# Turning the first x block by DMA in single tiles, with the v rows of wqkv on the other DMA queue, v of eight tiles tile by tile, and wk turned in two parts

## The chip, the core and the metric

The kernel runs on one core of a Trainium2 chip. The metric is device time in microseconds (us); a figure for a kernel is the median of its runs.

"Turn" below means a DMA that transposes on its way (DMA_TRANSPOSE in the profile). A "tile" of x is 128 tokens by 640 values, 160 KB. A "v piece" is 128 rows of the 640 v columns of wqkv, also 160 KB; v of one token tile needs all five pieces. SP is the sync engine, whose queue issues most DMAs.

## The reference

```python
def reference(A_x, A_wqkv, A_w_phi, A_wo, B_x, B_w_gate, B_w_up, B_w_down, gate_w):
    # S = 2048 tokens, D = 640, 32 heads of 20, F = 1728, all bf16
    def _A_ref(x, wqkv, w_phi, wo):
        ...                                   # q, k, v = x @ wqkv
        pq = jnp.einsum("bhsd,hdf->bhsf", q, w_phi)
        pk = jnp.einsum("bhsd,hdf->bhsf", k, w_phi)
        phi_q = concatenate([softmax(pq), softmax(-pq)])
        phi_k = concatenate([softmax(pk), softmax(-pk)])
        ...                                   # linear attention, then @ wo
    def _B_ref(x, w_gate, w_up, w_down):
        return (_gelu(x @ w_gate) * (x @ w_up)) @ w_down
    x = A_x
    g = _sigmoid((x * gate_w).sum(-1, keepdims=True))
    return g * _A_ref(x, A_wqkv, A_w_phi, A_wo) + (1 - g) * _B_ref(x, ...)
```

(Shortened; the attention's den has a term of 1e-6.) Only the first 30 of some 290 us matter here: x has to be turned, so that the model dimension lies on partitions; v is x times the v columns of wqkv; and the kernel folds w_phi into wk and wq, for which it needs those turned too.

## The kernel before

A small scheduler issues instructions in program order on each engine and adds the semaphore waits. The loads at the start, with cuts:

```python
    def loads(self):
        ...
        def xload(q, j):      # two tiles of x, tokens on partitions, as they lie in memory
            sc.dma(q, lambda e: e.dma_start(self.xtok[:, j:j + 2, :], x4[:, j:j + 2, :]), ...)
        def wload(T, c0, key):
            sc.dma("sp", lambda e: e.dma_start_transpose(T[:, :, :], self.wqkv[:, c0:c0 + D]), writes=[key])
        def xturn(t, n):
            a, z = t * P, (t + n) * P
            sc.dma("sp", lambda e: e.dma_start_transpose(self.xT[:, :, a:z], self.x[a:z, :]), ...)
        ...
        xload("sp", 0)
        xload("act", 2)
        ...                                            # wphi, on act
        for kt in range(KD):                           # the five v pieces
            sc.dma("sp", lambda e: e.dma_start(self.w3[:, kt, 0:D], w3[:, kt, 2 * D:3 * D]), writes=[("wv", kt)])
        ...                                            # gate column, on act
        xturn(4, 2)
        wload(self.wkT, D, "wkT")
        xturn(6, 2)
        wload(self.wqT, 0, "wqT")
        xturn(8, 4)
        xturn(12, 4)
        ...                                            # then the FFN weights
```

The first four tiles of x are turned by the PE, and their v is computed piece by piece: the first v piece for all four tiles, then the second, and so on, so that the last piece is needed last.

```python
    def attention_state(self):
        ...
        warm(7)                                        # dummy matmuls on a zeroed tile
        xt(0, 6, "d"); xt(1, 7, "a"); xt(2, 2, "d"); xt(3, 3, "a")   # PE transposes, evacuated by DVE or ACT
        for t in range(4): vs(t, 0)                    # vs(t, kt): v piece kt for tile t
        ...                                            # the same for pieces 1, 2, 3
        self.blockdiag()
        self.gate_column(6)
        for t in range(4):
            vs(t, 4)
            ...                                        # evacuations
        f = self.fold
        self.v_early(4, 6)                             # all five pieces for one tile
        self.v_early(5, 0)
        f(0, "k", (2, 3), "d")                         # fold of wk: needs the turned wk
        f(1, "k", (4, 5), "a")
        self.v_early(6, 6)
        f(2, "k", (2, 3), "d"); f(3, "k", (4, 5), "a"); f(4, "k", (0, 1), "d")
        self.v_early(7, 6)
        self.k_early(0, 2)
        f(0, "q", (4, 5), "d")                         # fold of wq: needs the turned wq
        ...
        self.pq(0, 1, 1); self.pq(0, 0, 0); self.pq(0, 3, 3)         # bank 6 + n % 2
        ...
```

The softmax here doesn't subtract the row's maximum and nothing guards it: scores larger than these inputs give would overflow.

## Time and profile before

| | before |
|---|---|
| time | 289.78 us, median of 3 (289.63 to 290.26); 289.85 with three more |
| span of the profiled run | 288.7 us |
| first fold of wk / of wq on the PE | 15.25 / 20.98 us |
| v pieces land (five) | 5.3, 6.4, 6.8, 7.2, 7.7 us |
| turned wk / wq lands | 12.2 / 18.9 us |

Landing times are the start of a DMA's issue plus the time from issue to landing that the profile gives for it, good to about 0.1 us.

The profile page, its first lines: busy us of each engine, share of the span, instructions.

```profile
span 288.7 us, 7036 instructions
PE 284.0 (98%) x3032; PEld 190.1 (66%) x3032; DVE 166.7 (58%) x337; ACT 105.1 (36%) x199; POOL 27.6 (10%) x52
```

The PE is busy nearly everywhere and nothing else bounds the kernel, so what counts in the start is when the PE gets through it. The PE's timeline of the start (start us, duration us, engine, line, operation, out<-in, count, and in brackets the idle time before and what ended it):

```profile
4.72 2.31 PE L290 MATMUL ps<-ident,xtok 128*128 128x128 bf16 x20 [0.30 <-DMA xtok<-in_A_x_dram]
6.82 4.73 PE L363 MATMUL ps<-w,xT 128*128 128x480 bf16 x32
...
11.45 1.25 PE L363 MATMUL ps<-w,xT 128*128 128x480 bf16 x8
12.53 2.88 PE L351 MATMUL ps<-w,xT 128*128 128x512 bf16 x20
15.25 0.79 PE L331 MATMUL ps<-BD,wkT 128*128 128x140 bf16 x12
...
20.98 0.79 PE L331 MATMUL ps<-BD,wqT 128*128 128x140 bf16 x12
```

L290 are the PE transposes, L363 v of tiles 0 to 3, the twenty at 12.53 v of tiles 4 and 5, L331 the folds. The last has 2.0 us to spare on the turned wq.

The timeline of the sync queue (the duration is the time the queue needs to issue):

```profile
0.80 0.41 SPq L216 DMA_DIRECT2D xtok<-in_A_x_dram  x1
1.27 2.43 SPq L233 DMA_DIRECT2D w<-in_A_wqkv_dram  x5
3.75 2.11 SPq L224 DMA_TRANSPOSE xT<-in_A_x_dram  x1
5.91 3.71 SPq L220 DMA_TRANSPOSE wkT<-in_A_wqkv_dram  x1
9.66 1.41 SPq L224 DMA_TRANSPOSE xT<-in_A_x_dram  x1
11.11 4.25 SPq L220 DMA_TRANSPOSE wqT<-in_A_wqkv_dram  x1
```

It has no pause: everything that is turned stands in one line, and wq comes after 9 blocks of 160 KB.

The table of stretches (us from:to, length; busy us and instructions of each engine; then the recorded PE clock, the DMA engines' busy share, GB/s). The share sums the times of all packets that start in the stretch, so it can exceed 1. The clock column reads 1.00 also where a trace holds no clock record, as this one: its 480-column matmuls took 524 ns at 6.82 us and 366 ns from 7.25 us, so the clock was not full before about 7 us.

```profile
core 0: us, PE busy (x) PEld busy (x) DVE busy (x) ACT busy (x) POOL busy (x), PEclk, DMA share, GB/s
2.00:4.00 2.00, 2.00 (x6) 0.59 (x4) 0.00 (x0) 1.28 (x1) 1.52 (x11) 1.00 0.95 325
4.00:6.00 2.00, 1.70 (x14) 1.29 (x14) 0.49 (x1) 0.00 (x0) 1.59 (x12) 1.00 1.09 323
6.00:8.00 2.00, 2.00 (x17) 1.42 (x16) 1.47 (x6) 1.41 (x2) 1.12 (x8) 1.00 1.23 224
```

Plain loads move 325 GB/s until 6 us. The waits of the PE near 29 us (waiting engine, for what: total us, times, longest):

```profile
PE ps L351 <- ACT Eq L518: 0.3, 1, 0.3
```

That is a q projection that waits for PSUM bank 7.

### The profile page before, as it was taken

The page shows a single profiled execution, that of the slowest core. Times are in us where ns is not written, and L with a number is a line of the kernel's source. Part 1 is how long each engine was busy: PE and PEld are TensorE (multiplying, and loading weights), DVE is VectorE, ACT ScalarE, POOL GpSimd, SP SyncE. Part 2 cuts the span into 40 slices and gives each one's busy share as a digit, 9 for nine tenths or more (in the row PEclk, how much of TensorE's full clock was granted, in tenths as well). Part 3 has the DMA queues.
Part 4 walks back from the last instruction along what each step waited for, and adds up shares of the span by engine and source line. Part 5 has one row for each costly group of instructions (what it writes and reads, how often), then busy time and mean ns, then how long its engine had stood idle before and what let it go on. Part 6 is the DMA issues. An engine that isn't in the chain of part 4 may idle for free.

```text
span 288.7 us, 7036 instructions
## 1 busy us (share of the span) xinstructions
PE 284.0 (98%) x3032; PEld 190.1 (66%) x3032; DVE 166.7 (58%) x337; ACT 105.1 (36%) x199; POOL 27.6 (10%) x52
## 2 busy tenths in 40 slices
PE   7999999999999999999999999999999999999996
PEld 4576689999994444444688744457764444777785
DVE  2338999999977553777776443326744232674001
ACT  2357897687663322322111332220132222022111
POOL 7000000000000000111113200001230000113000
DMA  8999994000002000011212120000312000031211
GB/s 225 217 192 293 361 356 119 0 2 2 0 2 48 0 0 0 3 25 31 25 37 70 28 66 0 3 0 15 80 25 68 0 2 0 2 92 26 70 49 49
DMA packets 36938, 18.68 MB, mean 65 GB/s; under 512 B 28970, under 2 KB 36394, under 8 KB 36906
## 3 DMA queue, kind: packets, MB, share of 16 engines
q1 hardware_dynamic: 36096, 17.86, 23.8%
q8 instruction: 24, 0.39, 0.6%
q10 hardware_dynamic: 810, 0.35, 0.5%
q14 instruction: 8, 0.07, 0.1%
HBM read 9.04 MB, written 2.62 MB: 40 GB/s over the span
## 4 chain that ended last, share of the span: by engine, by line
PE 97%; DMA 1%; ACT 1%; issue 0%; ACTq 0%
PE ps L351 61%; PE ps L708 28%; PE ps L651 2%; PE ps L363 2%; PE ps L449 2%; DMA xtok<-in_A_x_dram 1%; PE ps L331 1%; PE ps L290 1%; ACT Ek L413 0%; ACT Eq L518 0%; ACT outsb L721 0%; ACT gcol L416 0%; PE ps L313 0%; ACTq L42 0%
## 5 line engine op out<-in xcount | busy, mean ns | idle before, releaser
L708 PE MATMUL ps<-wd_sb,hT 64*128 64x320 bf16 (+2 forms) x918 | 67.6, 288 | 0.0
L625 DVE TENSOR_TENSOR hT<-ps,gl 128x512 bf16<-128x512 f32 x52 | 35.7, 690 | 55.1 <-PE ps L351 54.9
L351 PE MATMUL ps<-xT,wg_sb 128*128 128x512 bf16 (+1 forms) x270 | 64.9, 379 | 0.0
L351 PE MATMUL ps<-xT,wu_sb 128*128 128x512 bf16 (+1 forms) x270 | 64.8, 379 | 0.0
L623 ACT ACTIVATE gl<-ps 128x512 bf16<-128x512 f32 x52 | 30.9, 597 | 71.5 <-PE ps L351 64.9
L708 PEld LDWEIGHTS ps<-wd_sb,hT 64*128 64x128 bf16 x918 | 46.0, 94 | 13.2 <-ACT gl L623 0.8
L351 PEld LDWEIGHTS ps<-xT,wu_sb 128*128 128x128 bf16 (+1 forms) x270 | 26.5, 99 | 29.7 <-DVE hT L625 0.4
L680 POOL TENSOR_TENSOR Og<-O,O 128x640 bf16<-128x640 bf16 x16 | 22.3, 1395 | 237.3 <-DVE O L678 237.3
L351 PEld LDWEIGHTS ps<-xT,wg_sb 128*128 128x128 bf16 (+1 forms) x270 | 25.9, 99 | 28.7 <-issue 0.5
L351 PE MATMUL ps<-w,xT 128*64 128x512 bf16 (+6 forms) x400 | 42.1, 325 | 0.0
L721 ACT ACTIVATE outsb<-ps,Gm 128x320 bf16<-128x320 f32 (+2 forms) x31 | 14.6, 516 | 74.8 <-PE ps L708 74.8
L351 PEld LDWEIGHTS ps<-w,xT 128*64 128x64 bf16 (+1 forms) x400 | 35.9, 107 | 4.7
L708 PE MATMUL ps<-wo_sb,goT 64*128 64x320 bf16 (+2 forms) x340 | 28.2, 288 | 0.0
L351 PE MATMUL ps<-xT,wq 128*64 128x512 bf16 (+1 forms) x185 | 26.4, 380 | 0.3 <-ACT Eq L518 0.3
L433 DVE TENSOR_TENSOR Ek<-Ek,Dk 128x640 bf16<-128x640 bf16 x32 | 25.0, 821 | 0.5
L678 DVE TENSOR_TENSOR O<-ps,RH 128x640 bf16<-128x640 f32 x32 | 24.8, 815 | 0.0
L424 DVE TENSOR_REDUCE Dk<-Ek 128x64 f32<-128x1280 bf16 x16 | 23.7, 1478 | 0.2 <-ACT gcol L416 0.2
L518 ACT ACTIVATE Eq<-ps 128x512 bf16<-128x512 f32 x40 | 21.7, 604 | 1.1 <-PE ps L351 0.8
L413 ACT ACTIVATE Ek<-ps 128x640 bf16<-128x640 f32 x32 | 20.7, 702 | 3.5 <-PE ps L351 3.5
L708 PEld LDWEIGHTS ps<-wo_sb,goT 64*128 64x128 bf16 x340 | 17.7, 94 | 4.7
L351 PEld LDWEIGHTS ps<-xT,wq 128*64 128x64 bf16 (+1 forms) x185 | 15.3, 108 | 3.5 <-ACT Eq L518 0.8
L667 DVE RECIPROCAL RH<-ps 128x32 f32<-128x32 f32 x16 | 5.7, 358 | 18.3 <-PE ps L651 18.3
(65 smaller groups left out, 151.1 us busy)
## 6 DMA issues: line engine op xcount, KB each, us to landing
out_dram<-outsb SPq DMA_DIRECT2D x7, 320.0 KB, 2.4
wd_sb<-in_B_w_down_dram SPq DMA_DIRECT2D x1, 2080.0 KB, 13.6
wg_sb<-in_B_w_gate_dram SPq DMA_DIRECT2D x1, 1120.0 KB, 6.0
wu_sb<-in_B_w_up_dram SPq DMA_DIRECT2D x1, 1120.0 KB, 8.5
wg_sb<-in_B_w_gate_dram SPq DMA_DIRECT2D x1, 960.0 KB, 9.7
wu_sb<-in_B_w_up_dram SPq DMA_DIRECT2D x1, 960.0 KB, 10.2
w<-in_A_wqkv_dram SPq DMA_DIRECT2D x5, 160.0 KB, 4.4
wo_sb<-in_A_wo_dram SPq DMA_DIRECT2D x1, 800.0 KB, 9.4
```

The lines of the kernel that those rows point to most:

```text
L351: self.sc.op("pe", lambda e: e.matmul(self.ps[a:z, bank * 512 + c0:bank * 512 + c0 + n], lhs[:, a:z], rhs, start=first, stop=fin), reads=r ...
L363: sc.op("pe", lambda e, c0=c0, n=n, bk=bk, col=col: e.matmul(self.bank(bk)[:, col:col + n], self.xT[:, kt, t * P:(t + 1) * P], self.w3[:, ...
L413: self.sc.op("act", lambda e, s=s, scale=scale: e.activation(self.Ek[:, se, s, :], self.ps[:, o:o + self.D], AF.Exp, scale=scale), reads=[ ...
L424: sc.op("dve", lambda e: e.tensor_reduce(self.Dk[:, se, 0, :].rearrange("p (s h) -> p s h", h=H), self.Ek[:, se, :, :].rearrange("p s (h d ...
L433: sc.op("dve", lambda e, v=v, r=r: e.tensor_tensor(v, v, r, ALU.mult), reads=[("Rk", se)], writes=[("Ek", se, s)])
L518: sc.op("act", lambda e, s=s, scale=scale: e.activation(self.Eq[:, s, i, b * self.BT:(b + 1) * self.BT], self.bank(bank), AF.Exp, scale=sc ...
L623: sc.op("act", lambda e: e.activation(self.gl[:, slot, :], self.bank(banks[0]), AF.Gelu_apprx_tanh), reads=[("ps", banks[0])], writes=[("g ...
L625: sc.op("dve", lambda e: e.tensor_tensor(hT[:, c, :], self.bank(banks[1]), self.gl[:, slot, :], ALU.mult), reads=[("ps", banks[1]), ("gl", ...
L678: dve(lambda e, o=o, f=f, s=s: e.tensor_tensor(o, V[s][:, :, :, 0:DH], f, ALU.mult), rb + [key(6 + s)], [("O", s, sl)], guard=old)
L680: sc.op("pool", lambda e: e.tensor_tensor(self.Og[:, sl, :], self.O1[:, sl, :], self.O2[:, sl, :], ALU.add), reads=[("O", 0, sl), ("O", 1, ...
L708: sc.op("pe", lambda e: e.matmul(self.bank(bk, w), lhs, rhs, start=opens and x == 0, stop=end and not opens, skip_group_check=True), reads ...
L721: sc.op("act", lambda e: e.activation(dst, self.bank(bk, w), AF.Copy, scale=g), reads=rd, writes=wr)
```

## The change

The intent: take the PE transposes and their evacuations (2.31 us of PE time) out of the start by letting the DMA turn the first x tiles too, singly so that the first arrives early; load the v pieces from the ACT queue at the same time; and split wk's turn so that x tiles 6 and 7 come between its parts. One early q projection also moves from PSUM bank 7 to bank 0. The diff, cut to its core (removed helpers, an order of memsets, an output layout, the number of semaphores of the ACT queue and book-keeping keys are left out):

```diff
-        xload("sp", 0)
-        xload("act", 2)
+        for kt in range(KD):
+            sc.dma("act", lambda e: e.dma_start(self.w3[:, kt, 0:D], w3[:, kt, 2 * D:3 * D]), writes=[("wv", kt)])
         ... wphi, on act
-        for kt in range(KD):
-            sc.dma("sp", lambda e: e.dma_start(self.w3[:, kt, 0:D], w3[:, kt, 2 * D:3 * D]), writes=[("wv", kt)])
         ... gate column, on act
+        xturn(0, 1)
+        xturn(1, 1)
+        xturn(2, 2)
         xturn(4, 2)
-        wload(self.wkT, D, "wkT")
+        wload(self.wkT, D, "wkT", 0, 2)
         xturn(6, 2)
-        wload(self.wqT, 0, "wqT")
+        wload(self.wkT, D, "wkT", 2, 5)
+        wload(self.wqT, 0, "wqT", 0, 5)
 ...
-        warm(7)                    # on a tile that the DVE clears first
-        xt(0, 6, "d")  ...         # PE transposes of tiles 0 to 3
-        for t in range(4): vs(t, 0)  ...
+        for i in range(8):         # dummy matmuls on the constant ones
+            sc.op("pe", lambda e: e.matmul(self.bank(7), ones[:, 0:P], ones, start=True, stop=True), writes=[("ps", 7)])
+        f = self.fold
         self.blockdiag()
+        for t in range(5):
+            self.v_early(t, 2 * t % 8)
+        self.gate_column(2)
+        self.v_early(5, 6)
 ...
-        self.pq(0, 3, 3)
+        self.pq(0, 3, 3, 0)
```

More of the change, by code (lines that the diff above doesn't have):

```diff
@@ L135, in run @@
         self.columns = False
-        self.sc = _Sched(nc, {"sp": (nc.sync, 16), "act": (nc.scalar, 4), "pool": (nc.gpsimd, 2)})
+        self.sc = _Sched(nc, {"sp": (nc.sync, 16), "act": (nc.scalar, 8), "pool": (nc.gpsimd, 2)})
         self.loads()
@@ L156, in alloc @@
         self.ident = T("ident", [P, P], BF16)
-        self.zero = T("zero", [P, 512], BF16)
         self.gz = T("gz", [P, P], BF16)
@@ L194, in alloc @@
         place([
-            [("xtok", [P, self.TB, D], BF16), ("wkT", [P, KD, D], BF16), ("wqT", [P, KD, D], BF16)],
+            [("wkT", [P, KD, D], BF16), ("wqT", [P, KD, D], BF16)],
             [("goT", [P, 8, KD, P], BF16), ("O1", [P, 2, D], BF16), ("O2", [P, 2, D], BF16),
@@ L211, in loads, with wload @@
         w3 = self.wqkv.rearrange("(kt p) n -> p kt n", p=P)
-        x4 = self.x[0:self.BT, :].rearrange("(p j) n -> p j n", j=self.TB)
-        def xload(q, j):
-            sc.dma(q, lambda e: e.dma_start(self.xtok[:, j:j + 2, :], x4[:, j:j + 2, :]),
-                   writes=[("xtok", j), ("xtok", j + 1)])
-        def wload(T, c0, key):
-            sc.dma("sp", lambda e: e.dma_start_transpose(T[:, :, :], self.wqkv[:, c0:c0 + D]), writes=[key])
+        def wload(T, c0, key, a, z):
+            sc.dma("sp", lambda e: e.dma_start_transpose(T[:, :, a * P:z * P], self.wqkv[a * P:z * P, c0:c0 + D]),
+                   writes=[(key, k) for k in range(a, z)])
         def xturn(t, n):
@@ L273, in loads @@
                 [("mask", i)])
+        for s in range(self.NSV):
+            pool(lambda e, s=s: e.memset(self.vaug[:, s, :, DH:self.DA], 1.0), [("vone", s)])
         for r in (0, 1):
@@ L282, in loads @@
                 channel_multiplier=-1), [("hmask", r)])
-        for s in range(self.NSV):
-            pool(lambda e, s=s: e.memset(self.vaug[:, s, :, DH:self.DA], 1.0), [("vone", s)])
-    def x_transpose(self, t, b, ek):
-        sc = self.sc
-        pv = self.bank(b).bitcast(BF16)
-        for c in range(self.KD):
-            sc.op("pe", lambda e, c=c: e.transpose(
-                pv[:, c * P:(c + 1) * P], self.xtok[:, t, c * P:(c + 1) * P], self.ident[:, :]),
-                reads=[("xtok", t), "ident"], writes=[("ps", b)], signal=(c == self.KD - 1))
-        out = self.xT[:, :, t * P:(t + 1) * P]
-        src = pv[:, 0:self.D].rearrange("p (c t) -> p c t", t=P)
-        if ek == "a":
-            sc.op("act", lambda e: e.activation(out, src, AF.Copy), reads=[("ps", b)], writes=[("xT", t)])
-        else:
-            sc.op("dve", lambda e: e.tensor_copy(out, src), reads=[("ps", b)], writes=[("xT", t)])
     def blockdiag(self):
@@ L333, in fold @@
                     start=first, stop=fin, skip_group_check=True),
-                    reads=["w%sT" % which, ("BD", i)], writes=[("ps", b)], signal=fin)
+                    reads=[("w%sT" % which, kt), ("BD", i)], writes=[("ps", b)], signal=fin)
         src = self.pair(banks)
@@ L358, in proj @@
                     kt == self.KD - 1, [("xT", t)] + [(k, kt) if k != "wgate" else k for k in keys])
-    def v_step(self, t, kt):
-        sc = self.sc
-        for c0, n, bk, col in ((0, 480, t, 0), (480, 160, 4 + t // 3, 160 * (t % 3))):
-            sc.op("pe", lambda e, c0=c0, n=n, bk=bk, col=col: e.matmul(
-                self.bank(bk)[:, col:col + n], self.xT[:, kt, t * P:(t + 1) * P], self.w3[:, kt, c0:c0 + n],
-                start=(kt == 0 and col == 0), stop=(kt == self.KD - 1), skip_group_check=True),
-                reads=[("xT", t), ("wv", kt)], writes=[("ps", bk)], signal=(kt == self.KD - 1))
-    def v_first_evac(self, ts, ek, tail):
-        sv, nt = ts[0], len(ts)
-        h0, nh = (24, 8) if tail else (0, 24)
-        dst = self.vaug[:, sv:sv + nt, h0:h0 + nh, 0:self.DH]
-        bk = 4 + ts[0] // 3 if tail else ts[0]
-        src = self.bank(bk, nt * nh * self.DH).rearrange("p (t h d) -> p t h d", t=nt, d=self.DH)
-        rd = [("ps", bk)] + [("vone", t) for t in ts]
-        wr = [("vaug", t) if tail else ("vmain", t) for t in ts]
-        if ek == "d":
-            self.sc.op("dve", lambda e: e.tensor_copy(dst, src), reads=rd, writes=wr)
-        else:
-            self.sc.op("act", lambda e: e.activation(dst, src, AF.Copy), reads=rd, writes=wr)
     def k_early(self, t, b0):
@@ L509, in kv_mask, with pq @@
                 self.kvk[i, r].append(("KV", i, r, g))
-    def pq(self, b, i, n):
+    def pq(self, b, i, n, bank=None):
         sc = self.sc
-        bank = 6 + n % 2
+        bank = 6 + n % 2 if bank is None else bank
         for kt in range(self.KD):
@@ L535, in attention_state @@
         sc = self.sc
-        sc.op("dve", lambda e: e.memset(self.zero[:, :], 0.0), writes=["zero"])
-        def warm(n):
-            for i in range(n):
-                sc.op("pe", lambda e: e.matmul(self.bank(0), self.zero[:, 0:P], self.zero[:, :], start=True, stop=True),
-                      reads=["zero"], writes=[("ps", 0)])
-        vs, ve, xt = self.v_step, self.v_first_evac, self.x_transpose
-        warm(7)
-        xt(0, 6, "d")
-        xt(1, 7, "a")
-        xt(2, 2, "d")
-        xt(3, 3, "a")
-        for t in range(4):
-            vs(t, 0)
-        for t in range(4):
-            vs(t, 1)
-        for t in range(4):
-            vs(t, 2)
-        for t in range(4):
-            vs(t, 3)
-        self.blockdiag()
-        self.gate_column(6)
-        for t in range(4):
-            vs(t, 4)
-            ve([t], "ad"[t % 2], False)
-            if t == 2:
-                ve([0, 1, 2], "a", True)
-        ve([3], "d", True)
-        f = self.fold
-        self.v_early(4, 6)
-        self.v_early(5, 0)
+        ones = self.nc.const_aps.tensor(1.0, [P, 512], BF16)
+        for i in range(8):
+            sc.op("pe", lambda e: e.matmul(self.bank(7), ones[:, 0:P], ones, start=True, stop=True), writes=[("ps", 7)])
+        f = self.fold
+        self.blockdiag()
+        for t in range(5):
+            self.v_early(t, 2 * t % 8)
+        self.gate_column(2)
+        self.v_early(5, 6)
         f(0, "k", (2, 3), "d")
         f(1, "k", (4, 5), "a")
-        self.v_early(6, 6)
+        self.v_early(6, 0)
         f(2, "k", (2, 3), "d")
         f(3, "k", (4, 5), "a")
-        f(4, "k", (0, 1), "d")
-        self.v_early(7, 6)
+        f(4, "k", (6, 7), "d")
+        self.v_early(7, 0)
         self.k_early(0, 2)
@@ L644, in num @@
         DB, DH = self.DB, self.DH
-        old = [("xtok", k) for k in range(4)] + ["wkT", "wqT"]
+        old = [(w, k) for w in ("wkT", "wqT") for k in range(self.KD)]
         w = self.HB * DB
@@ L727, in evac @@
                 return
-            if t0 < self.TB:
-                rows = self.out[0:self.BT, :].rearrange("(p j) n -> p j n", j=self.TB)[:, t0:t0 + 2, :]
-            else:
-                rows = self.out[t0 * P:(t0 + 2) * P, :].rearrange("(j p) n -> p j n", p=P)
+            rows = self.out[t0 * P:(t0 + 2) * P, :].rearrange("(j p) n -> p j n", p=P)
             sc.dma("sp", lambda e: e.dma_start(rows[:, :, c0:c1], self.outsb[:, os_:os_ + 2, c0:c1]),
```

## The prediction

> **What bounds the kernel.** The tensor engine. The page gives PE busy for 284.0 of 288.7 us, and the chain of waits is 97% PE. The change touches only the first 30 us, so it is worth how much earlier, or later, the PE finishes the start; the rest is carried along.
>
> **The start before** (timeline). Warm-up matmuls run 1.25 to 4.42 us. The first x rows land at 4.67 (issued 0.80, 3.87 us in the chain). Twenty PE transposes take 4.72 to 7.03 (2.31 us). v of tiles 0 to 3 ends at about 12.5, v of tiles 4 and 5 at 15.4. The turned wk is first used at 15.2 (landed 12.2), the turned wq at 20.98 (landed 18.9). The sync queue issues without a pause from 0.80 to 22.6 us. At 28.96 to 29.30 the PE waits 0.34 us for an Eq exponential that still holds PSUM bank 7.
>
> **Removed.** The 2.31 us of PE transposes, four evacuations of 0.49 to 0.70 us, and the 0.34 us wait (that projection goes to bank 0, free about 1 us sooner).
>
> **Added or moved.** Four x tiles come by DMA transpose, issued at 0.70 to 1.05 us a tile (the two-tile ones took 1.41 and 2.11). The five v loads (2.43 us of issue) go to the ACT queue and start 0.5 us earlier. Sync loses 2.84 us of issue and gains 2.8 to 4.2 us, so wq lands between 18.9 and 20.3. The Trainium skill, DMA: Bandwidth & Descriptors, "Issuing engines are not separate DMA queues", says a second queue saves only issue time because the DMA engines are shared; the windows table shows them full (DMA share about 1 from 2 us on), so I expect no extra bandwidth.
>
> **When v can start.** One x tile and all five v pieces, 960 KB, must land, where 640 KB were needed before. At the 325 GB/s of 2 to 4 us, with the same 1.2 us before the first byte and about 0.6 us of completion, that is an estimated 5.5 us. Six v tiles at 1.44 us then end at about 14.3, 1.1 us earlier, if the clock is fast.
>
> **The clock takes part of it back.** The PE transposes filled time in which the PE was slow: the 480-column matmuls show 445 ns at first and 363 ns from about 7.3 us. The skill, TensorE: Matmul & The Clock Gate, Part 1, puts the release after a busy window of about 3.4 us, free-running. Here it came 6 us after the first matmul. Now the warm-up ends at about 4.4 and the PE then waits about 1 us. If the release stays at 7.3, v loses about 0.8 of the 1.1; if the gap delays it by a window, some 1.5 us more; if it comes at 4.5, nothing.
>
> **Sum.** v about -0.5 (from -1.6 to +1.2), bank 0 -0.3, the folds of wk and wq 0 to +0.5 (wq's slack of 2 us shrinks). Predicted 289.0 us, range 287.6 to 290.3. Chances: faster by over 2% 0.01, within 2% 0.98, slower by over 2% 0.01.
>
> **What would show it.** v of tile 0 starting at 5 to 6 us, after an idle of about 1 us released by a DMA; v of tile 5 ending at 14 to 16; 512-column matmuls long until about 7 us; no PE wait for Eq near 29 us; later stages equal in length and only shifted.
>
> **What would make it wrong.** x transposes landing at 7 us or later because their small packets share engines with the v rows; a PE wait for wk or wq over 1 us; the clock released a window later; or v starting under 5 us, which gives over 2 us.

## More of the kernel before

The v pieces stand ahead of all turns.

## The result, and the profile after

The changed kernel took 291.03 us (290.55 to 292.51, 6 runs) against 289.85 for the kernel before in the same rounds: 1.2 us slower, ratio 1.0049 (95% interval 1.0025 to 1.0072). A ratio is the mean time of one kernel's fast runs over that of the other's of the same rounds, so not quite the ratio of the quoted medians. A second set of runs, in a later session (experiment 5), gave 1.0080 (1.0064 to 1.0097), so the loss is 1.2 to 2.5 us.

| | before | after |
|---|---|---|
| span of the profiled run | 288.7 us | 290.2 us |
| first x tile, turned, ready for the PE | 6 us (by the PE) | 4.9 us |
| v pieces land | 5.3, 6.4, 6.8, 7.2, 7.7 us | 3.2, 4.6, 6.3, 8.4, 8.7 us |
| first fold of wk | 15.25 us | 17.76 us |
| turned wq lands | 18.9 us | 23.2 us |
| first fold of wq | 20.98 us | 23.49 us |

The page:

```profile
span 290.2 us, 6993 instructions
PE 284.5 (98%) x3013; PEld 188.2 (65%) x3013; DVE 164.1 (57%) x331; ACT 104.8 (36%) x198; POOL 27.5 (9%) x52
```

The PE timeline:

```profile
4.90 1.03 PE L333 MATMUL ps<-w,xT 128*128 128x512 bf16 x2 [0.48 <-DMA xT<-in_A_x_dram]
6.30 0.39 PE L333 MATMUL ps<-w,xT 128*128 128x512 bf16 x1 [0.37 <-DMA w<-in_A_wqkv_dram]
8.48 8.03 PE L333 MATMUL ps<-w,xT 128*128 128x512 bf16 x47 [1.79 <-DMA w<-in_A_wqkv_dram]
...
17.76 0.79 PE L313 MATMUL ps<-BD,wkT 128*128 128x140 bf16 x12
...
23.49 0.79 PE L313 MATMUL ps<-BD,wqT 128*128 128x140 bf16 x12
```

v starts early, at 4.90 us, does two matmuls, then waits for the third piece, then for the fourth. From there 47 matmuls take 8.03 us; in a trace below in which the clock stays up they take 6.31. The sync queue:

```profile
0.80 8.13 SPq L218 DMA_TRANSPOSE xT<-in_A_x_dram  x4
8.97 1.47 SPq L213 DMA_TRANSPOSE wkT<-in_A_wqkv_dram  x1
10.48 1.76 SPq L218 DMA_TRANSPOSE xT<-in_A_x_dram  x1
12.28 2.08 SPq L213 DMA_TRANSPOSE wkT<-in_A_wqkv_dram  x1
14.41 5.07 SPq L213 DMA_TRANSPOSE wqT<-in_A_wqkv_dram  x1
```

The turn of wq is issued 3.3 us later than before, and lands 4.3 us later. The stretches:

```profile
2.00:4.00 2.00, 2.00 (x6) 0.60 (x4) 0.00 (x0) 0.00 (x0) 1.53 (x11) 1.00 1.02 282
4.00:6.00 2.00, 1.45 (x3) 0.13 (x2) 0.00 (x0) 0.00 (x0) 1.78 (x14) 1.00 0.94 156
6.00:8.00 2.00, 0.39 (x1) 0.10 (x1) 0.00 (x0) 0.00 (x0) 0.84 (x5) 1.00 1.30 175
8.00:10.00 2.00, 1.52 (x10) 0.74 (x11) 0.00 (x0) 0.53 (x1) 0.00 (x0) 0.83 1.32 193
10.00:12.00 2.00, 2.00 (x10) 1.12 (x9) 1.18 (x5) 1.46 (x2) 0.00 (x0) 0.50 1.14 249
```

Two things stand out. From 4 to 8 us the DMA engines are full and move about six tenths of what they moved before (156 and 175 GB/s against 323 and 224). And the PE clock, recorded in the column before the DMA share, is at half from 10 to 12 us. In stretches of 1 us it reads 0.66 at 9 to 10 and 0.63 at 12 to 13, so half clock lasted from about 9.3 to 12.7 us. The two queues apart, from 2 to 8 us (packets, MB, share of the 16 engines' time); q10 is the ACT queue with the v pieces, q1 the sync queue with the turns:

```profile
q10 hardware_dynamic: 704, 0.79, 59.8%
q1 hardware_dynamic: 1755, 0.43, 48.5%
```

So the v pieces got some 132 GB/s, and the turns beside them 72. The waits of the first 40 us (PEld is the weight load, which waits along with the matmul):

```profile
PEld ps L333 <- DMA w<-in_A_wqkv_dram: 3.5, 3, 2.1
PE ps L333 <- DMA w<-in_A_wqkv_dram: 2.2, 2, 1.8
PE ps L333 <- DMA xT<-in_A_x_dram: 0.5, 1, 0.5
```

The wait for Eq near 29 us is gone, as forecast. After that the two traces run in parallel: the last evacuation of the program starts at 285.99 us before and at 288.06 after. That is 2.07 us, of which the spans show 1.5, because the last store landed in 1.6 us and not in 2.3. In the traces of this study that store took 1.6 to 2.7 us; why is open, and nothing is built on it.

### The profile page after: what moved, and what is told of

Its sections match the earlier page's. It is cut to its first block, busy times and chain, and to the rows that moved or that the text cites. A ratio compares the mean times of both kernels' runs of the same rounds, so it can differ in the third digit from the quotient of the medians.

```text
span 290.2 us, 6993 instructions
## 1 busy us (share of the span) xinstructions
PE 284.5 (98%) x3013; PEld 188.2 (65%) x3013; DVE 164.1 (57%) x331; ACT 104.8 (36%) x198; POOL 27.5 (9%) x52
## 4 chain that ended last, share of the span: by engine, by line
PE 96%; DMA 2%; ACTq 0%; ACT 0%; issue 0%
PE ps L333 63%; PE ps L647 28%; PE ps L590 2%; DMA w<-in_A_wqkv_dram 2%; PE ps L410 2%; PE ps L313 1%; ACTq L222 0%; ACT outsb L660 0%; PE ps L295 0%
## 5 line engine op out<-in xcount | busy, mean ns | idle before, releaser
L333 PE MATMUL ps<-w,xT 128*64 128x512 bf16 (+6 forms) x440 | 50.1, 329 | 2.6 <-DMA w<-in_A_wqkv_dram 2.2
L333 PEld LDWEIGHTS ps<-w,xT 128*64 128x64 bf16 (+1 forms) x440 | 39.2, 107 | 12.7 <-DMA w<-in_A_wqkv_dram 3.5
L366 ACT ACTIVATE vaug<-ps 128x640 bf16<-128x640 f32 x16 | 11.3, 707 | 14.4 <-PE ps L333 13.7
## 6 DMA issues: line engine op xcount, KB each, us to landing
wd_sb<-in_B_w_down_dram SPq DMA_DIRECT2D x1, 2080.0 KB, 13.4
```

What stands on the lines that cost most here:

```text
L333: self.sc.op("pe", lambda e: e.matmul(self.ps[a:z, bank * 512 + c0:bank * 512 + c0 + n], lhs[:, a:z], rhs, start=first, stop=fin), reads=r ...
L366: self.sc.op("act", lambda e: e.activation(self.vaug[:, sv, :, 0:self.DH], self.bank(B, self.D).rearrange("p (h d) -> p h d", d=self.DH), ...
```

## The experiments

The rivals at the outset: (S) the v pieces come late because they now share the DMA engines with the turns, where they had been ahead of them in one queue; (C) the PE's idle time let its clock fall, and the slow stretch is most of the loss; (W) the turned wq, at the end of a longer line of turns, holds the PE whatever the v stage does; and (M), which came up on the way, that turns are a special poison for loads beside them. Each comparison in percent is with the kernel before, run in the same rounds.

**1. v pieces ahead of the turns again** (changed kernel, `sc.dma("act", ... ("wv", kt))` to `sc.dma("sp", ...)`).

> The changed kernel with one edit: the five v pieces are issued first on the sync queue, ahead of the x turns, so that the turns start about 2.5 us later and the v pieces have the DMA engines nearly to themselves. Theory S (v pieces and x turns share the DMA engines, and each v piece waits for turn packets): the fifth v piece lands at 5.5 to 6.5 us (8.6 in the changed kernel), 3 to 3.6 us after its issue instead of 6; the first x tile lands at 6.5 to 7.5; v of tile 0 starts there and waits for no v piece; v of tile 5 ends at 15 to 17 instead of 17.9; time 289.0 to 290.5. Rival R (v pieces are slow for another reason, such as the shape of their rows or the memory): the fifth v piece still needs about 6 us and lands at 8 or later.

Measured: v pieces at 3.2 to 6.3 us, the first x tile at 6.9, v from 7.00 us without a wait for a v piece, the first fold of wk at 16.71 us (17.76 in the changed kernel). So order decides when the pieces land. But the time is 290.99, ratio 1.0060 (1.0040 to 1.0079), outside what I expected: the x turns start later in turn, and the turned wq lands at 22.9 us. The clock came up late as well: the six 512-column matmuls from 7 to 10 us took 624 ns each on average, those after that about 378.

```profile
PE ps L333 <- DMA xT<-in_A_x_dram: 2.6, 1, 2.6
PE ps L313 <- DMA wqT<-in_A_wqkv_dram: 0.3, 1, 0.3
```

The PE waits 2.6 us for x and then for wq: moving the pieces ahead cures one lateness and leaves the other.

**2. Dummy matmuls in the gaps** (changed kernel; eleven more dummies before the third and fourth piece, one more at the start).

```diff
+        for kt in range(self.KD):
+            fill((0, 0, 2, 9, 0)[kt])
+            self.mm(0, 0, 512, self.xT[:, kt, 0:P], self.w3[:, kt, 0:512], ...)   # v of tile 0, piece kt
```

> The changed kernel with 12 further dummy matmuls that keep the PE busy from 4.4 to about 8.5 us, in the gaps where it waits for x and v pieces. Theory C (the idle of 6.7 to 8.5 us made the clock fall to half from 9.3 to 12.7 us, which cost about 1.5 us): no stretch at half clock after 9 us, v of tiles 1 and 2 takes 1.4 us each instead of 2.7 and 1.8, v of tile 5 ends at 16.3 to 16.9 instead of 17.9. The turned wq lands at 23.2 in the changed kernel and its fold would now be wanted at 22, so most of the gain at that point turns into a PE wait for wq of about 1 us and the time falls only by 0.2 to 0.6 us. Rival (the clock in the trace is only a record, the delay is all DMA): v of tile 5 still ends at 17.5 or later.

Measured: no stretch at half clock after 6.7 us; the first fold of wk at 16.34 us instead of 17.76. Groups by shape in the stretch 10 to 12 us (count | busy us, mean ns of one | idle before), first the changed kernel, then this one:

```profile
L333 PE MATMUL ps<-w,xT 128*128 128x512 bf16 x5 | 2.5, 631 | 0.0
```

```profile
L333 PE MATMUL ps<-w,xT 128*128 128x512 bf16 x9 | 2.3, 378 | 0.0
```

So the clock is real. The same 47 matmuls take 8.03 us in the changed kernel and 6.31 here, 1.7 us less; as the last dummies hold them up by 0.3 us, 1.4 us of the v stage is gained. But the first fold of wq starts at 22.31 us, just as the turned wq lands (13.97 + 8.3), and its weight load waits 0.4 us for it. The time is 291.28, ratio 1.0060 (1.0037 to 1.0083): no gain that shows, where I expected 0.2 to 0.6 us. The changed kernel was not run beside it, and its own ratio was 1.0049 in one set and 1.0080 in another, so a gain of that size could hide. In two of the six runs (291.21 us with a span of 289.0, 291.56 with 289.4) time and span lie 2.2 us apart, in the others 1.2 to 1.3; time and trace do not tell quite the same there.

**3. The queue of the v pieces alone** (kernel before; the five v loads issued on the ACT queue behind its half of x; x still loaded plainly and turned by the PE).

> The kernel before with one edit: the five v pieces go to the ACT queue behind half of x, so nothing but x is ahead of the turns on the sync queue and they start at about 1.2 us beside the v pieces; x tiles 0 to 3 are still transposed by the PE. Theory S: the v pieces are slowed although x is loaded plainly: the fifth lands at 8.5 to 10 us (about 7.7 before), the PE waits for v pieces 1 us or more in tiles 0 to 3, v of tile 5 ends at 15.8 to 17, time 290 to 291.5. Rival T (only the turning of the first x tiles matters, the queue of the v pieces does not): v pieces land as before, no PE wait for them, time within 0.3 us of the kernel before.

Measured: 292.60 us, ratio 1.0112 (1.0082 to 1.0143), 3.2 us slower, more than the whole change and more than I expected. The pieces land at 6.2, 9.9, 10.4, 11.0 and 11.8 us, the first fold of wk starts at 18.81.

```profile
4.00:6.00 2.00, 1.88 (x15) 1.47 (x15) 0.49 (x1) 0.78 (x1) 1.59 (x13) 1.00 1.00 160
6.00:8.00 2.00, 1.80 (x15) 1.13 (x14) 0.49 (x1) 1.80 (x3) 1.09 (x8) 1.00 1.13 108
```

Same bytes as before, same instructions; with the v pieces beside the turns instead of ahead of them the engines move 160 and 108 GB/s instead of 323 and 224. (S) holds with x tiles 0 to 3 loaded plainly. The clock is recorded at half here too, from 10.0 to 13.4 us, after the PE had waited 1.7 us for a v piece. The queue reached the turn of wq at 13.9 us instead of 11.1, so the turns lost too.

**4. PSUM bank 0 alone** (kernel before; `self.pq(0, 3, 3)` to `self.pq(0, 3, 3, 0)`), run in two sets.

> The kernel before with the fourth early q projection in PSUM bank 0 instead of 7, as in the changed kernel. The PE wait of 0.34 us at 29 us goes, the time falls by 0.3 us (289.5). Rival: the PE is held a few us later by another wait for an exponential or for the normalised k and nothing is gained.

> The kernel before with PSUM bank 0 once more, to stand beside the next kernel on the same chip: 0.3 to 0.9 us below the kernel before.

Measured: 288.68 us, ratio 0.9968 (0.9947 to 0.9989), then 289.32, ratio 1.0001 (0.9983 to 1.0018). The wait for Eq is gone in both traces; in time one set shows 0.9 us (by the ratio) and the other nothing, and it can't be told better.

**5. Both suspected limits, one at a time and together**: the changed kernel again; the same with wq loaded plainly (meant to give a wrong result); and that with the dummies of experiment 2.

```diff
-        wload(self.wqT, 0, "wqT", 0, 5)
+        sc.dma("sp", lambda e: e.dma_start(self.wqT[:, :, :], w3[:, :, 0:D]), ...)   # not turned
```

> The changed kernel itself once more, so that the next kernels stand beside it on the same chip: 1.2 to 1.6 us slower than the kernel before.

> The changed kernel with wq loaded plainly instead of turned; its result is wrong on purpose, its instructions and waits are otherwise the same. Theory of two limits (the v stage, and the turned wq that lands at about 23.2 us, each by itself put the first fold of wq at about 23.4): with the v stage as late as before, the fold still starts at about 23.4 and nothing or at most 0.3 us is gained against the changed kernel. Rival (wq alone is the limit): 1 us or more is gained.

> Both limits taken away: the dummy matmuls that keep the clock up, and wq loaded plainly (wrong result on purpose). Theory of two limits: the first fold of wq starts at 21.8 to 22.2 us with no wait for wq (22.3 with the dummies alone), and the time is 1.2 to 1.8 us below the changed kernel, within 0.6 us of the kernel before. What is left to the kernel before is that v pieces land late. Rival (something after the folds takes the time): the time stays within 0.5 us of the changed kernel.

| kernel | time, us | ratio to before | first fold of wk / wq, us |
|---|---|---|---|
| changed again | 291.76 | 1.0080 (1.0064 to 1.0097) | 18.45 / 24.18 |
| + wq plain | 291.28 | 1.0077 (1.0056 to 1.0097) | 18.00 / 23.73 |
| + wq plain + dummies | 290.38 | 1.0042 (1.0027 to 1.0058) | 16.38 / 22.12 |

The changed kernel was 2.5 us slower here, where I expected 1.2 to 1.6. With wq plain the ratio hardly moves, but this is a weak test of (W): the plain wq landed at 21.2 us and the turned one at 21.4, 2.8 us before its fold, so there was no wait to take away. With the clock kept up as well, 1.4 us come back; the dummies without the plain wq were not run in this set, so what wq adds to that is not shown. In this trace of the changed kernel no clock was recorded, and the clock column reads 1.00 throughout, but the 512-column matmuls of 10 to 12 us took 634 ns, as slow as at half clock: here the clock seems never to have come up before. What remains, 1.2 us to the kernel before, stands already at the first fold of wk (16.38 against 15.25 in the first trace), from v pieces that came late; I had expected 0.6 or less.

**6. x in pairs instead of singles** (changed kernel; `xturn(0, 2)` for `xturn(0, 1)` and `xturn(1, 1)`).

> The changed kernel with x tiles 0 to 3 turned in two pairs instead of two singles and a pair. Theory I (one turn holds the sync queue about 1.25 us whether it has one tile or two): the queue reaches the turn of wq about 1.2 us earlier, at 13.0 to 13.5 us instead of 14.4 to 14.7; the first x lands a little later (5 to 6 us), the v pieces still land at 8 to 9 us and bound the start, so the time stays within 0.5 us of the changed kernel. Rival (the issue time goes with the tiles): wq is reached at the same time as in the changed kernel.

Measured: 294.21 us, ratio 1.0171 (1.0155 to 1.0187). The expectation failed. A pair is indeed issued in as little time as a single tile (1.37 us against 1.32), but the queue reached wq at 14.9 us, no earlier, because the following turns were held back (3.42 and 3.41 us for two blocks each, against 1.41 and 2.11 us for two in the kernel before; the changed kernel itself has 3.65 and 1.47). And the fourth and fifth v pieces landed at 10.2 and 10.8 us: more turned bytes in flight early, more delay.

```profile
PE ps L332 <- DMA w<-in_A_wqkv_dram: 2.8, 1, 2.8
PE ps L332 <- DMA xT<-in_A_x_dram: 1.4, 1, 1.4
```

The 46 matmuls after that wait took 9.03 us, so the slow clock is in this loss too. The single tiles, which I had taken for an expense, seem to shield the v pieces.

**7. No turns at all** (changed kernel; all turns of x, wk and wq replaced by plain loads of as many bytes, wrong result).

> The changed kernel with every turn of x, wk and wq replaced by a plain load of the same number of bytes into the same place, in the same order on the same queue (wrong result on purpose; runs of 256 bytes for one x tile, more for the larger ones; wk and wq take their bytes from wo). Theory M (turns in flight slow the v pieces; bytes and the second queue do not): the five v pieces land by 7 us (8.4 to 8.9 in the changed kernel) with no wait of the PE over 0.7 us after the first x tile, although the sync queue sends its bytes faster than before; v of tile 5 ends at 13.5 to 15.5 us, the folds follow without a wait, and the time is 2 us or more below the changed kernel, below the kernel before too. Rival B (any 160 KB a microsecond on the other queue does it): the v pieces still land at 8 us or later.

Measured: 292.07 us, ratio 1.0096 (1.0068 to 1.0123). The v pieces land at 3.1, 4.5, 6.4, 8.3 and 9.1 us, no earlier than in the changed kernel. Theory (M) falls, and rival B holds: plain loads on the other queue delay the v pieces just as much. The first four are issued faster (0.62 to 0.84 us each), so more of their bytes are in flight.

```profile
6.00:8.00 2.00, 0.39 (x1) 0.10 (x1) 0.00 (x0) 0.00 (x0) 0.86 (x5) 0.79 1.06 317
8.00:10.00 2.00, 1.51 (x7) 0.73 (x8) 0.00 (x0) 0.00 (x0) 0.00 (x0) 0.50 1.23 275
```

The engines move 317 and 275 GB/s, not 175 and 193; turns do lower the rate. But of the bytes that move, the v pieces get only a share. The two queues from 2 to 8 us, as for the changed kernel above:

```profile
q1 hardware_dynamic: 2372, 0.86, 54.9%
q10 hardware_dynamic: 884, 0.80, 42.1%
```

The v pieces got 133 GB/s, as beside the turns (132), while twice as many bytes passed on the other queue (143 GB/s against 72). So turns are not the only loads that do this, but a turned byte cost its neighbours about as much as two plain ones. Half clock lasted from about 7.1 to 14.0 us here.

**8. v pieces on the ACT queue, with the sync queue held back** (experiment 3; the first turn waits for all five v pieces).

```diff
-        xturn(4, 2)
+        sc.dma("sp", lambda e: e.dma_start_transpose(self.xT[:, :, 4 * P:6 * P], self.x[4 * P:6 * P, :]),
+               reads=[("wv", k) for k in range(KD)], writes=[("xT", 4), ("xT", 5)])
```

> The kernel before with the v pieces on the ACT queue (which was 3.2 us slower, v pieces landing at 9.9 to 11.8 us), and the sync queue made to wait for the fifth v piece before its first turn. Theory P (what counts is that nothing else is in flight beside the v pieces, not which queue they are on): the five v pieces land by 7 us, the PE does not wait for them, v of tile 3 ends at 12 to 13 us as in the kernel before; the turns start at 6 to 7 us instead of 3.8, so the turned wq lands at 21 to 22.5 and the time is 0.5 to 2 us over the kernel before. Rival (the ACT queue is slower by itself): v pieces still land at 9 us or later.

Measured: the pieces land at 4.9, 6.4, 6.9, 7.3 and 7.8 us, as in the kernel before, from the ACT queue. From 4 to 6 us that queue had the engines nearly to itself and moved 0.68 MB, some 340 GB/s. It is not the queue that is slow, it is what is in flight beside it. The time is 292.28, ratio 1.0107 (1.0066 to 1.0147), more than expected: the turns, begun at 7.9 us, are now so late that the PE waits 1.9 us for wk and 0.6 us for x.

**9. The four extra turns alone** (kernel before; x tiles 0 to 3 also turned into a spare tile, behind the v pieces).

```diff
+        for a, z in ((0, 1), (1, 2), (2, 4)):
+            sc.dma("sp", lambda e: e.dma_start_transpose(self.spare[:, :, a * P:z * P], self.x[a * P:z * P, :]), ...)
         xturn(4, 2)
```

> The kernel before with one thing added: x tiles 0 to 3 are also turned, behind the v pieces on the sync queue, into a spare tile that nothing reads. Theory T (the changed kernel's four more turned tiles alone cost over 1 us, as wk and wq are turned later): the v pieces land as before (5.3 to 7.7 us), turns of x tiles 4 to 7, wk and wq come 3.5 to 4.5 us later, the turned wq lands at 22.4 to 23.4 instead of 18.9, the PE waits about 0.5 to 2 us for turned x, wk or wq tiles, the first fold of wq starts at 22.3 to 23.4 instead of 20.98, and the time is 1 to 2.4 us over the kernel before. Rival (the slack of wq covers it): under 0.5 us.

Measured: 292.93 us (292.57 to 296.66), ratio 1.0150 (1.0084 to 1.0216). The v pieces land as before (5.3 to 7.4 us); the queue reaches the turn of wq at 16.0 instead of 11.1 us, and wq lands at 23.4.

```profile
PE ps L335 <- DMA wkT<-in_A_wqkv_dram: 2.6, 1, 2.6
PE ps L355 <- DMA xT<-in_A_x_dram: 1.5, 2, 0.9
```

I expected 1 to 2.4 us and got 3.1: here wk is not split, and the PE waits for wk and x; it does not wait for wq, which (W) is about. The profiled run was the slowest, with a slow clock again after these waits; its first fold of wq at 27.75 us overstates the others.

**10. The order of v alone** (kernel before; tiles 0 to 7 one by one, each with all five pieces).

> The kernel before (x loaded plainly and turned by the PE, v pieces on the sync queue, seven warm-up matmuls) with only the order of v changed: tiles 0 to 7 one after another, each with all five v pieces, as in the changed kernel. Theory O (the order costs only as far as the last v piece comes late): the fifth piece lands at 7.7 us as before, so the PE waits under 0.8 us for it in tile 0, the first fold of wk starts at 15.2 to 16.0 us (15.25 before) and the time is within 0.7 us of the kernel before. Rival (the order is a main cost): the first fold starts at 16.5 us or later, time over 1 us more.

Measured: the first fold of wk at 14.62 us, no later than before; weight loads wait 0.6 us in all for v pieces. 290.04 us, ratio 1.0030 (1.0007 to 1.0052), 0.8 us where I expected 0.7 at most. The order is not a main cost while the pieces come in time; what it costs with late pieces, as in the changed kernel, was not tested; whether the 0.3% belongs to it the trace doesn't show.

**11. Versions meant to beat both.** The kernel before with bank 0, x loaded plainly in four single tiles on the two queues, and six dummies on the constant ones; then the same with the change's split of wk.

```diff
-        xload("sp", 0)
-        xload("act", 2)
+        xload("sp", 0)            # one tile each
+        xload("act", 1)
+        xload("sp", 2)
+        xload("act", 3)
```

> A version meant to beat both: the kernel before, with PSUM bank 0 for the fourth early q projection, x loaded plainly in four single tiles on the two queues (two loads of two tiles before) and turned by the PE, and six warm-up matmuls on the constant ones from 0.84 us instead of seven on a cleared tile from 1.25 us. Plain loads run beside plain loads only, so the first x tile should land at 3.2 to 3.6 us instead of 4.7, the PE transposes end at 5.6 to 6.2 instead of 7.0, v begins as the first v piece lands (about 5.7), and the fold of wq is wanted at 20.0 to 20.4, still after wq has landed (18.9 to 19.3). Time 0.6 to 1.4 us below the kernel before. Rival: the start is bound by the v pieces or by the slow clock, and no more than the 0.4 us of bank 0 is gained.

> The kernel with x loaded plainly in single tiles and bank 0 (which waited 0.88 us for the turned x tiles 6 and 7 at 15.9 us), with one part of the change added: wk is turned in two parts, with x tiles 6 and 7 between them. Theory Q (the queue of turns is the next limit, and its order decides): x tiles 6 and 7 land at 13.5 to 14.5 us, the wait for them goes, the first fold of wq starts at 20.0 to 20.4 (or at the landing of wq, 19.5 to 20.4) instead of 21.0, and the time is 0.5 to 1.0 us below that kernel and 0.5 to 1.0 below the one with bank 0 alone. Rival: the wait only moves to the second part of wk or to wq, and the fold of wq starts at 20.8 or later; no gain.

Measured: 288.55 us, ratio 0.9979 (0.9965 to 0.9993); with the split 288.88, ratio 0.9986 (0.9969 to 1.0002). The first started the folds of wk at 14.22 us, a full us earlier than the kernel before, and then gave nearly all of it back:

```profile
15.89 1.53 PE L352 MATMUL ps<-w,xT 128*128 128x512 bf16 x10 [0.88 <-DMA xT<-in_A_x_dram]
```

x tiles 6 and 7 were still being turned behind wk, and the first fold of wq came at 21.00 us, no earlier than before. With wk split, that wait is gone and the fold starts at 20.28 us. In time that gain of 0.7 us does not show clearly: the interval of the second reaches just past 1. Both are faster than the changed kernel; over the kernel before the gain is about 0.2%, certain only for the first. Of 0.5 to 1.0 us expected from the split, 0.4 was seen against the kernel of experiment 4 beside it. Both kernels contain bank 0, for which experiment 4 saw up to 0.3% by itself, so a gain beyond bank 0 is not shown in time.

## Why the prediction was wrong

The prediction of 289.0 us (287.6 to 290.3) was missed: the time is 291.03, and the sign was wrong.

**The step that failed** is, in its words, "One x tile and all five v pieces, 960 KB, must land ... At the 325 GB/s of 2 to 4 us ... that is an estimated 5.5 us." The x tile did land at 4.9 us. The fourth and fifth v piece landed at 8.4 and 8.7, about 3 us after the estimate. The sum counted only the bytes that the PE wanted, and gave them the whole rate. But on a second queue nothing keeps the other bytes behind: the turns of x tiles 1 to 5 were issued from 2.2 us on and took their part. By 8 us the engines had moved 1,226 KB (282 x 2 + 156 x 2 + 175 x 2), at half the assumed rate after 4 us, and the five v pieces were still not all there. At 325 GB/s those bytes would have been moved by about 5.8 us (an estimate from these two numbers), so here the fallen rate weighs more than the added bytes; in experiment 7, at 277 GB/s over the same 6 us, it was more the bytes. Experiments 3 and 7 show the lateness with x tiles 0 to 3 loaded plainly and without turns, and experiments 1 and 8 take it away by ordering alone. The sum also counted one x tile only: tile 1 landed at 8.8 us and tiles 2 and 3 at 10.7, where v at the predicted 1.44 us a tile from 5.5 us on would have wanted them at about 6.9, 8.4 and 9.8. So by this estimate v pieces in time would not have been enough. The Trainium skill, DMA: Bandwidth & Descriptors, "Queues, rings and completion order", says that each DMA engine goes round robin over the queue rows it has work for, packet by packet. The trace agrees so far that both queues were served side by side (0.21 MB for the v pieces and 0.10 for the turns from 4 to 6 us, 0.18 and 0.17 from 6 to 8); the turn-taking itself no run here shows. I had cited its neighbour section for "no extra bandwidth", which the runs confirm (1.23 MB from 2 to 8 us against 1.74 before), and overlooked the consequence: two queues give no extra bandwidth, and they give up the order.

**The clock** was weighed rightly in kind, and a loss of the size of the worse branch happened. The prediction had "if the gap delays it by a window, some 1.5 us more". In the second trace it came up late: 512-column matmuls took 606 to 635 ns from 5.25 to 13.0 us. In the first it had come up (390 ns at 6.30 and 8.48 us) and fell again at 9.3 us, after a pause of 1.79 us in which the PE waited for a v piece. The prediction had only one wait, of about 1 us, for x; so in that trace the clock's loss followed from the late pieces. Experiment 2 gives 1.4 us (17.76 to 16.34), or 1.7 by the length of the 47 matmuls. The skill, TensorE: Matmul & The Clock Gate, Part 1, speaks of a free-running window of 3,413 ns; half clock lasted 3.4 us in the changed kernel (9.3 to 12.7) and 6.8 us in experiment 7 (7.14 to 13.97), one and two such windows.

**The v term**, "about -0.5 (from -1.6 to +1.2)", measured +2.5 us (first fold of wk 15.25 to 17.76). Against the 14.3 us estimated at full clock, late pieces made about 2.0 (16.34), the clock 1.4; without the 0.3 us of the dummies it is 1.7 each.

**The turns.** "Issued at 0.70 to 1.05 us a tile" was too low for singles: 1.25 and 1.32 us, nearly the price of a pair (1.41). "wq lands between 18.9 and 20.3" came out as 23.2 in the first trace and 21.4 in the second. In the first trace its slack of 2.0 us was nearly used up: it landed 0.2 us before its weight load (23.38), and the PE did not wait for it only because v was just as late. There the two losses lie side by side and do not add; once v is earlier, as in experiments 1 and 2, weight loads wait 0.6 and 0.4 us for wq. In the second trace wq landed 2.8 us before its fold and was no limit. That mending one lateness returned little in time (experiments 1 and 2) fits this, but how much of it is due to wq is not shown. Experiment 9 shows that the extra turns alone cost about 3 us, there by way of wk and x.

**Right**: the PE bounds, and later stages are only shifted; the wait for Eq goes (its -0.3 us was neither confirmed nor refuted in time); v of tile 0 starts after a wait for a DMA; and one of the named ways to be wrong, the clock a window later, was one of the causes in kind. The start itself, at 4.90 us, was by the prediction a sign of a gain of over 2 us ("v starting under 5 us"); it was none, as the first x tile says nothing of the fourth and fifth v piece.

What stays open: how the 1.2 to 2.5 us divide between late pieces and late wq to better than half a us; why the last store takes 1.6 us in some traces and 2.7 in others; and why experiment 3 loses more than the whole change: its wk turn was one long transfer in flight beside the v pieces, and its clock was at half for 3.4 us, but neither was tested alone.

## What to carry to other kernels

A single DMA queue is also an order of importance: loads that are needed first are protected by standing first, and moving them to a second queue puts them in competition with everything that the first queue then issues sooner. Before costing a start by bytes over bandwidth, list all that is in flight by then, not only what is awaited. And where several late arrivals lie close together, find each one's own landing time, since removing the one that the profile names may only uncover the next. A pause of the PE for late data can also cost clock on top: in the changed kernel 3.4 us at half clock followed a pause of 1.79 us.

## What the Trainium skill lacked or had wrong

- DMA: Bandwidth & Descriptors, "Issuing engines are not separate DMA queues", says a second issuing engine only saves issue time. It lacks that it can cost: the same five loads landed at 5.3 to 7.7 us ahead of the turns in one queue and at 6.2 to 11.8 us beside them on another, and the kernel lost 3.2 us (experiment 3). The queue that had some 340 GB/s nearly alone (experiment 8) got 132 beside turns and 133 beside plain loads.
- Advanced Engine Details and Errata, "X-Bar Transpose (TRN2)", says that transpose DMAs are as fast as regular ones. Here the DMA engines moved 323 to 325 GB/s with plain loads and 220 to 276 GB/s with turns alone (kernel before, 8 to 12 us); mixed with plain loads from another queue, 108 to 175 GB/s (changed kernel and experiment 3).
- No page has the price at the issuing queue of a turn of this size on this chip: 1.25 to 1.32 us for a tile of 128 x 640, 1.37 us for two tiles first in line (experiment 6) and 1.41 us behind the turn of wk (kernel before), up to 3.85 us for two tiles while v pieces ran beside them (second trace of the changed kernel).
- TensorE: Matmul & The Clock Gate, Part 1, warns that clock records are not to be fully trusted. The second trace of the changed kernel bears it out: it has no clock record, and the column reads 1.00, where 512-column matmuls took 634 ns, against 378 ns at full clock. The length of matmuls is the safer sign.
